# Prologue order, weight loads in pieces, one joint last projection and a mask moved between engines, in a recurrent-memory transformer kernel

## The chip, the core and the metric

The kernel runs on one core of a Trainium2 chip. A core has a matrix engine (TensorE, PE in the profile, whose weight loads are shown as PEld), VectorE (DVE), ScalarE (ACT), GpSimd (POOL) and SyncE (SP), which only issues transfers here. They run side by side and wait for each other by semaphores. The metric is the device time in microseconds (us) of one execution; smaller is better.

## The reference

The input x has 2048 tokens of width 448, in 64 segments of 32 tokens. Two layers of the same kind follow each other, each with a recurrent attention A and a gated feed-forward B:

```python
for s in range(n_seg):                               # A, 64 segments in order
    h = concat([mem, xs])                            # 8 memory rows + 32 tokens, L = 40
    q, k, v = h @ Wq, h @ Wk, h @ Wv                 # 16 heads of 256
    scores = q k^T * scale, masked (causal; the 8 memory keys are open to all)
    o = softmax(scores) v, then @ Wo                 # back to width 448
    mem = o[:8]; outs.append(o[8:])
# B: h = relu(x @ W_gate) * (x @ W_up); return h @ W_down     (448 -> 1792 -> 448)
x = x + A(layernorm(x)); x = x + B(layernorm(x))
x = x + A(layernorm(x)); x = x + B(layernorm(x))
```

The memory of a segment comes out of the one before, so the segments of a layer can't be done at once.

## The kernel before

**Prologue (lines 196 to 325).** For each pair of heads p (8 groups, `p4` of half `hf`) the products Wq Wk^T and Wv Wo are made once, as `A_sb` and `B_sb`. A block of 512 columns of Wq, Wk or Wv is loaded into one of six `nat` tiles by SP (`load_nat`), transposed on TensorE into `tpw` and copied to `qT`, `kT` or `vT` (`flips`, two halves for each). Copies out of PSUM are dealt out to VectorE and ScalarE by `share`. In the first loop over p each of the eight (kd, eo) positions has two `aps` products of 384 columns and two `mxw` products of 64, and the transposes for the next p (`todo`) are taken one by one after each kd, that is after positions 1, 3, 5 and 7 of 0 to 7. `first_rows` comes behind the third group. The second loop makes `B_sb` (`bps`). Behind it SP issues five loads of the feed-forward weights, `Wg_sb`, `Wu_sb` and `Wd_sb`.

**Steps (lines 505 to 661).** The layers are two chains of segments, the second `LAG` = 4 steps behind the first. `step(g)` handles segment g of chain 0 and segment g - 4 of chain 1, so steps 4 to 63 have both chains (full steps), 0 to 3 and 64 to 67 have one, and call 68 only projects. `xs` are the chains whose token output of the step before is projected in this step, `ms` those whose memory is needed next. A step projects its rows with `A_sb` (`prj`, evacuated to `TQ` and `TZ`), for the two halves of the heads, hf 0 and 1. The scores of the memory rows are `Sm`, those of the token rows `Sx`. The causal mask enters `Sx` as the first product of the accumulation:

```python
mm(Sp[:, :, :], ident[:], maskS[:], start=True, stop=False, skip_group_check=True)
```

`weights_of` makes the softmax on VectorE, with the exponential on ScalarE, out of `Sm` into `PM` and out of `Sx` into `PX`. `flipped` transposes those on TensorE (`pps`) and VectorE copies them to `PT`. `weigh_m` makes `ya` and `yb` from `PT` of the memory rows, `weigh_x` makes `y` from that of the token rows; both are evacuated to `Y`. `project_out` multiplies `Y` with `B_sb` into one PSUM tile `ox` of 80 columns, token rows of chain 0 in columns 0 to 31, memory in 32 to 47, token rows of chain 1 in 48 to 79, restricted to the columns `lo:hi` in use. It runs over t = 0 to 27 with four products each, and it is written in pieces between the other work:

```python
project_out(0, 0, 18)
probs_x(1, Sx1)
pm = flipped(PM[1], 1, "m1")
px0 = flipped(PX[0], 2, "x0")
project_out(0, 18, 21)
weigh_m(1, hk, pm)
```

Odd steps from 3 on also carry a feed-forward block (`Feed`: `residual`, `norm`, `xposed`, `gate_up` seven times, `down`, `norm2`, `feed_on`). Step 67 has chain 1 only and no `ms`: it projects the tokens of step 66, and call 68 those of step 67. `finish` copies the token columns of `ox` to `OT` and the memory back into `hT`. A last feed-forward block ends the kernel.

The order on TensorE is the order in which the program is written: `in_order` ties every matmul to the one before. The order on the other engines is made by the framework from the dependencies.

Of the kernel before, what the change touches and what calls it, by code (L numbers as in the profile page):

```python
# [23 lines left out]
FT = 14  # L24
# [8 lines left out]
HW = 4 * HI  # L33
W = 2 * L
XO = (0, 2 * L - SEG)
M0 = SEG
HX = (0, 64 + MEM)
HM = (SEG, 64)
# [15 lines left out]
def build_kernel(ctx, tc, A_x, A_mem0, A_Wq, A_Wk, A_Wv, A_Wo, B_W_gate, B_W_up, B_W_down, out,  # L54
# [141 lines left out]
    with tc.tile_pool(name="pre", bufs=6) as pre:  # L196
# [71 lines left out]
        for p in range(NP):  # L268
            hf, p4 = divmod(p, 4)
            qT, kT = ready  # L270
            ready, todo = queue(p + 1)
            mx_ps = psum.tile([P, 4, 128], F32, tag="ps", name="mxw")
            for kd in range(4):
                for eo in range(2):
                    aps = psum.tile([P, 3, 128], F32, tag="ps", name="aps")
                    for t in range(2):
                        e = 2 * eo + t
                        mm(aps[:, :, :], qT[:, e, kd * 128:(kd + 1) * 128],
                           kT[:, e, 0:384], start=(t == 0), stop=(t == 1))
                    for t in range(2):  # L280
                        e = 2 * eo + t
                        mm(mx_ps[:, kd, eo * 64:eo * 64 + 64], qT[:, e, kd * 128:(kd + 1) * 128],
                           kT[:, e, 384:448], start=(t == 0), stop=(t == 1))
                    t0 = eo * 4 + p4
                    if kd < 3:
                        share(A_sb[:, kd, hf, t0:t0 + 17:8, :], aps[:], 384, (1.28, 0.85))
                    elif upper(hf, eo):
                        share(A_sb[64:128, 3, hf, t0, :], aps[64:128, 0, :], 128, (1.28, 0.85))
                        share(A_sb[0:64, 3, hf, t0 + 8:t0 + 17:8, :], aps[0:64, 1:3, :], 256, (1.28, 0.85))
                    else:  # L290
                        share(A_sb[0:64, 3, hf, t0:t0 + 17:8, :], aps[0:64], 384, (1.28, 0.85))
                if todo:
                    todo.pop(0)()
            share(A_sb[:, 0:3, hf, 24 + p4, :], mx_ps[:, 0:3, :], 384, (1.28, 0.85))
            share(A_sb[0:64, 3, hf, 24 + p4, :], mx_ps[0:64, 3, :], 128, (1.28, 0.85))
            if p == 2:
                first_rows()
# [52 lines left out]
    Wg_sb = main.tile([P, 4, F], BF, name="Wg_sb")  # L350
    Wu_sb = main.tile([P, 4, F], BF, name="Wu_sb")
    Wd_sb = main.tile([P, FT, DM], BF, name="Wd_sb")
    for dst, src in ((Wg_sb, B_W_gate), (Wu_sb, B_W_up)):
        nc.gpsimd.memset(dst[64:128, 3, :], 0.0)
        nc.sync.dma_start(dst[:, 0:3, :], src[0:384].rearrange("(k p) n -> p k n", p=P))
        nc.sync.dma_start(dst[0:64, 3, :], src[384:448])
    nc.sync.dma_start(Wd_sb[:], B_W_down.rearrange("(f p) d -> p f d", p=P))

    class Feed:

# [115 lines left out]
    def queries(hf, g, kd):  # L476
        return TQ[hf][:, g, 2 * kd:2 * kd + 2, :] if kd < 3 else TZ[hf][:, g, :]

    def weights_of(Sp, n, dst, keep, tag):

        mx = main.tile([P, n], F32, tag=f"mx{tag}", name="mx")
        nc.vector.tensor_reduce(mx[:], Sp[:], axis=AX.X, op=ALU.max)
        se = main.tile([P, n, L], F32, tag=f"se{tag}", name="se")
        nc.vector.tensor_tensor(se[:], Sp[:], mx[:].unsqueeze(2).to_broadcast([P, n, L]), op=ALU.subtract)  # L484
        nc.scalar.activation(se[:], se[:], AF.Exp, scale=SCALE)  # L485
        ssum = main.tile([P, n], F32, tag=f"ssum{tag}", name="ssum")
        nc.vector.tensor_reduce(ssum[:], se[:], axis=AX.X, op=ALU.add)
        rs = main.tile([P, n], F32, tag=f"rs{tag}", name="rs")
        nc.vector.reciprocal(rs[:], ssum[:])
        if keep is not None:  # L490
            nc.vector.tensor_tensor(rs[:], rs[:], keep, op=ALU.mult)
        nc.vector.tensor_tensor(dst[:, :, 0:L], se[:], rs[:].unsqueeze(2).to_broadcast([P, n, L]), op=ALU.mult)
# [12 lines left out]
    def step(g, ff, pre):  # L505
# [4 lines left out]
        hb = hTb[gb % 2]  # L510
        cols = [(0, 32) if c == 0 else (48, 80) for c in xs] + [(32, 40) if c == 0 else (40, 48) for c in ms]
        lo, hi = min(a for a, _ in cols), max(b for _, b in cols)
        ox = psum.tile([P, 4, W], F32, tag="ox", bufs=1, name="ox")

        def hk_make():
            kps = psum.tile([P, 4, 128], BF, tag="ps", name="kps")
# [15 lines left out]

        def scores_x(hf):
            Sp = psum.tile([P, 4, L], F32, tag="ps", name="Sx")
            mm(Sp[:, :, :], ident[:], maskS[:], start=True, stop=False, skip_group_check=True)
            for half in range(2):
                for c in chains:
                    for kd in range(4):
                        mm(Sp[:, 2 * half + c, :], queries(hf, 3 * c + half, kd), moving(hb, j, kd, (c,)),
                           start=False, stop=(half == 1 and c == chains[-1] and kd == 3), skip_group_check=True)  # L540
            return Sp

        def probs_x(hf, Sp):
            weights_of(Sp, 4, PX[hf], None, f"x{hf}")

        def weigh_m(hf, hk, PT):
            if not ms:
# [11 lines left out]
        def weigh_x(hf, hk, PT, then=None):  # L559

            def keep(eng, c, t0, src):
                n = src.shape[-1] // SEG
                dst = YB[hf][:, t0:t0 + n, XO[c]:XO[c] + SEG]
                k = max(1, n // 8)
                evac(eng, dst.rearrange("p (k i) (e q) -> p k e i q", k=k, q=16),
                     src.rearrange("p (k e i q) -> p k e i q", k=k, e=2, q=16))

            y1 = {c: psum.tile([P, 512], F32, tag="ps", name=f"y1_{c}") for c in chains}
            for kd in range(2):
                for c in chains:  # L570
                    rows = slice(64 * c, 64 * c + L)
                    mm(y1[c][:, kd * 256:kd * 256 + 256], hk[rows, kd, :], PT[rows, 0:256], start=True, stop=True)
            for c in chains:
                keep(nc.scalar if c == 0 else nc.vector, c, 0, y1[c][:])
            y2 = {c: psum.tile([P, 384], F32, tag="ps", name=f"y2_{c}") for c in chains}
            for c in chains:
                rows = slice(64 * c, 64 * c + L)
                mm(y2[c][:, 0:256], hk[rows, 2, :], PT[rows, 0:256], start=True, stop=True)
            for eo in range(2):
                for c in chains:  # L580
                    rows = slice(64 * c, 64 * c + L)
                    mm(y2[c][:, 256:384], hk[rows, 3 + eo, :],
                       PT[rows, :].rearrange("p (e o w) -> p e o w", e=2, o=2)[:, :, eo, :],
                       start=(eo == 0), stop=(eo == 1))
            pre = then() if then is not None else {}
            for c in chains:
                keep(nc.scalar if c == 0 else nc.vector, c, 16, y2[c][:, 0:256])
                keep(nc.vector if c == 0 else nc.scalar, c, 24, y2[c][:, 256:384])
            return pre

        def project_out(hf, t0, t1):

            for t in range(t0, t1):
                for mc in range(4):
                    mm(ox[:, mc, lo:hi], B_sb[:, hf, t, mc * 128:(mc + 1) * 128],
                       YB[hf][:, t, lo:hi], start=(hf == 0 and t == 0 and mc == 0),
                       stop=(hf == 1 and t == NT - 1 and mc == 3), skip_group_check=True)

        def finish():
            if ms:  # L600
                src = ox[:, :, M0:M0 + 16].rearrange("p k (c m) -> p k c m", m=MEM)
                set_mem(g + 1, src[:, :, ms[0]:ms[-1] + 1, :], ms)
            o = (g - 1) % BLK * SEG
            for c in xs:
                o2 = o + (TB if c == 0 else 0)
                nc.scalar.copy(OT[:, :, o2:o2 + SEG], ox[:, :, XO[c]:XO[c] + SEG])
# [12 lines left out]
        project(0, chains, hb, j, (6, 0, 1), pre)  # L619
        if ff is not None:  # L620
            ff.residual()
        project(0, chains, hb, j, (2, 3, 4, 5))
        hk = hk_make()
        if ff is not None:
            ff.norm()
        project(1, chains, hb, j, (6, 0, 1))
        scores_m(0)
        project(1, chains, hb, j, (2, 3))
        if ff is not None:
            ff.xposed()  # L630
        project(1, chains, hb, j, (4, 5))
        pm = flipped(PM[0], 1, "m0")
        Sx0 = scores_x(0)
        weigh_m(0, hk, pm)
        scores_m(1)
        Sx1 = scores_x(1)
        probs_x(0, Sx0)
        feed(0, 1, 2)
        project_out(0, 0, 18)
        probs_x(1, Sx1)  # L640
        pm = flipped(PM[1], 1, "m1")
        px0 = flipped(PX[0], 2, "x0")
        project_out(0, 18, 21)
        weigh_m(1, hk, pm)
        feed(3, 4)
        project_out(0, 21, NT)
        feed(5, 6)
        weigh_x(0, hk, px0)
        if ff is not None:
            ff.down()  # L650
# [1 line left out]
        px1 = flipped(PX[1], 2, "x1")  # L652
        if ff is not None:
            ff.norm2()
        project_out(1, 16, 25)
        if ff is not None:
            ff.feed_on()
        project_out(1, 25, NT)
        finish()
        nxt = active(g + 1)  # L660
        return weigh_x(1, hk, px1, (lambda: project_early(nxt, hTb[(g + 1) // BLK % 2], (g + 1) % BLK)) if nxt else None)

# [75 lines left out]
```

## Time and profile before

| | |
|---|---|
| time, median of 3 runs | 1717.07 us (1716.97 to 1718.64) |
| profiled execution | 1716.17 us |
| span from its first to its last instruction | 1714.4 us |
| mean granted TensorE clock | 0.993 |
| matmuls | 41498 |
| DMA, mean | 33.17 MB, 19 GB/s |

The profile gives busy time of each engine, 40 slices of the span, the chain of work that ended last and groups of instructions. The trace can also be asked for stretches of time, for what each engine waited for, and for the instructions in order of time. "Waits for issue" are times in which an engine waited for nothing that the profile shows. A matmul's busy time holds its drain, which overlaps the next one, so its pace is read from the distance of two starts. The queues of the DMA part are q1 (hardware, issued by SP here), q0 (software, by POOL) and q8 and q14 (instructions).

### The profile page before, as it was taken

The numbers are of one execution on the slowest core, as the hardware profiler recorded it, in microseconds if no ns is written. First come the engines' busy times: TensorE is split into PE (matmuls) and PEld (weight loads), VectorE is DVE, ScalarE is ACT, GpSimd is POOL, SyncE is SP. The second block draws the span as 40 slices with busy tenths as digits, with TensorE's granted clock in tenths as the row PEclk, the third lists the DMA queues.
The fourth block names the chain that finished last, engine by engine and source line by source line (L and its number), as shares of the span: only waits on it lengthen the run. The fifth ranks groups of instructions, "written<-read, shape, count | busy, mean of one in ns | idle before, by whom it ended". The sixth has DMA issues, their size and how long they took to land.

```text
span 1714.4 us, 90663 instructions
## 1 busy us (share of the span) xinstructions
PE 1686.5 (98%) x41498; PEld 1589.5 (93%) x41498; DVE 1132.2 (66%) x3794; ACT 660.8 (39%) x1965; POOL 94.6 (6%) x202
## 2 busy tenths in 40 slices
PE   8989999999999999999999999999999999999998
PEld 6688999999999999999999999999999999999987
DVE  6656666676666666766666666766666667666664
ACT  5633333433333333343333334333333343433332
POOL 5300000000000000000000000000000000000000
PEclk9979999999999999999999999999999999999999
DMA  9520000000000000000000000000000000000000
GB/s 252 163 68 8 8 9 6 6 9 9 9 9 9 9 9 4 9 9 8 9 9 9 9 6 7 9 9 9 9 8 9 9 3 9 9 8 6 6 6 6
DMA packets 26623, 33.17 MB, mean 19 GB/s; under 512 B 3192, under 2 KB 24576, under 8 KB 26240
## 3 DMA queue, kind: packets, MB, share of 16 engines
q1 hardware_dynamic: 25152, 23.70, 5.0%
q8 instruction: 324, 5.31, 1.2%
q0 software_dynamic: 1088, 3.68, 0.7%
q14 instruction: 59, 0.48, 0.1%
HBM read 23.70 MB, written 1.84 MB: 15 GB/s over the span
## 4 chain that ended last, share of the span: by engine, by line
PE 96%; DVE 2%; issue 1%; ACT 1%; DMA 0%; POOL 0%; SPq 0%; POOLq 0%; DVEq 0%; ACTq 0%
PE ox L82 31%; PE prj L82 30%; PE ups L82 6%; PE gps L82 6%; PE dps L82 5%; PE y L82 4%; PE Sx L82 3%; PE pps L85 1%; PE bps L82 1%; PE tpw L85 1%; PE Sm L82 1%; PE aps L82 1%; PE ya L82 1%; PE tps L85 1%; PE yb L82 1%; PE kps L85 1%
## 5 line engine op out<-in xcount | busy, mean ns | idle before, releaser
L82 PE MATMUL ox<-Y,B_sb 128*128 128x80 bf16 (+4 forms) x15456 | 590.6, 199 | 1.5 <-issue 1.5
L82 PEld LDWEIGHTS <-B_sb 128*128 128x128 bf16 x15456 | 564.1, 99 | 10.2 <-issue 0.2
L82 PE MATMUL prj<-hT,A_sb 128*128 128x80 bf16 (+3 forms) x15232 | 569.5, 199 | 3.2 <-issue 3.2
L82 PEld LDWEIGHTS <-A_sb 128*128 128x128 bf16 (+1 forms) x15232 | 544.1, 99 | 7.8 <-issue 3.6
L89 ACT CAST TQ<-prj 128x320 bf16<-128x320 f32 (+1 forms) x456 | 169.9, 384 | 160.5 <-PE prj L82 128.5
L91 DVE CAST TQ<-prj 128x320 bf16<-128x320 f32 (+1 forms) x456 | 193.1, 431 | 44.9 <-PE prj L82 38.6
L91 DVE CAST Y<-y 128x128 bf16<-128x128 f32 (+2 forms) x384 | 162.2, 464 | 56.3 <-PE y L82 34.3
L89 ACT CAST Y<-y 128x512 bf16<-128x512 f32 (+2 forms) x384 | 144.2, 417 | 80.7 <-PE y L82 54.7
L396 DVE SCALAR_TENSOR_TENSOR hh<-gps,ut 128x256 bf16<-128x256 f32 (+1 forms) x238 | 95.6, 402 | 100.3 <-PE gps L82 93.6
L499 DVE COPY PT<-pps 128x128 bf16<-128x128 bf16 (+1 forms) x272 | 63.8, 255 | 120.2 <-PE pps L85 114.0
L82 PE MATMUL ups<-xT,Wu_sb 128*128 128x128 bf16 (+1 forms) x1904 | 140.0, 217 | 0.5 <-DVE xT L382 0.5
L82 PE MATMUL gps<-xT,Wg_sb 128*128 128x128 bf16 (+1 forms) x1904 | 140.0, 217 | 0.0
L395 ACT CAST ut<-ups 128x256 bf16<-128x256 f32 (+1 forms) x238 | 84.3, 355 | 105.5 <-PE ups L82 100.2
L557 ACT CAST Y<-yb 128x192 bf16<-128x192 f32 x134 | 42.6, 318 | 189.6 <-PE yb L82 189.0
L82 PEld LDWEIGHTS <-hk 40*128 40x128 bf16 (+1 forms) x1950 | 96.4, 95 | 16.9 <-issue 1.3
L82 PEld LDWEIGHTS <-Wg_sb 128*128 128x128 bf16 x1904 | 111.8, 98 | 0.0
L82 PEld LDWEIGHTS <-Wu_sb 128*128 128x128 bf16 x1904 | 109.5, 98 | 0.6 <-issue 0.6
L485 ACT ACTIVATE se<-se 128x80 f32<-128x80 f32 (+1 forms) x270 | 74.5, 299 | 90.0 <-DVE se L484 87.6
L160 POOL TENSOR_SCALAR rstd<-mv 128x1 f32<-128x1 f32 x67 | 14.8, 221 | 1554.1 <-DVE mv L158 1504.2
L82 PE MATMUL dps<-Wd_sb,hh 128*128 128x448 bf16 x476 | 95.9, 353 | 0.0
L82 PEld LDWEIGHTS <-TQ 128*128 128x128 bf16 x1938 | 86.8, 97 | 0.2 <-ACT TQ L89 0.2
L89 ACT CAST TZ<-prj 64x320 bf16<-64x320 f32 (+2 forms) x152 | 56.0, 378 | 74.2 <-DVE TZ L91 72.9
(112 smaller groups left out, 1801.1 us busy)
## 6 DMA issues: line engine op xcount, KB each, us to landing
wo<-in_A_Wo_dram POOLq DMA_DIRECT2D x8, 448.0 KB, 5.3
nat<-in_A_Wq_dram SPq DMA_DIRECT2D x8, 384.0 KB, 5.5
nat<-in_A_Wk_dram SPq DMA_DIRECT2D x8, 384.0 KB, 5.9
nat<-in_A_Wv_dram SPq DMA_DIRECT2D x8, 384.0 KB, 5.4
xa<-in_A_x_dram SPq DMA_DIRECT2D x32, 56.0 KB, 2.2
xa<-xp SPq DMA_DIRECT2D x32, 56.0 KB, 1.9
out_dram<-xa SPq DMA_DIRECT2D x32, 56.0 KB, 2.0
xp<-in_A_x_dram SPq DMA_DIRECT2D x30, 56.0 KB, 2.1
```

Source lines behind the costliest of these rows:

```text
L82: in_order(nc.tensor.matmul(*a, **k))
L85: in_order(nc.tensor.transpose(*a))
L89: nc.scalar.copy(dst, src)
L91: eng.tensor_copy(dst, src)
L160: nc.gpsimd.tensor_scalar(out=rstd[:], in0=mv[:, 1:2], scalar1=EPS, scalar2=None, op0=ALU.add)
L395: nc.scalar.copy(ut[:, :, n], ups[:, :, n])
L396: nc.vector.scalar_tensor_tensor(out=hh[:, 2 * u:2 * u + 2, n], in0=gps[:, :, n], scalar=0.0, in1=ut[:, :, n], op0=ALU.max, op1=ALU.mult)
L485: nc.scalar.activation(se[:], se[:], AF.Exp, scale=SCALE)
L499: nc.vector.tensor_copy(PT[:], pps[:].rearrange("p b q -> p (b q)"))
L557: nc.scalar.copy(YB[hf][:, 16:28, M0:M0 + 16], yb[:].rearrange("p (t q) -> p t q", q=16))
```

## The change

It has five parts.

- In the first prologue loop the transposes for the next group are taken after positions 0, 2, 4 and 5.
- The feed-forward weights are loaded in 15 pieces, `Wu_sb` first, each issued by `next_piece` from SP at five places of a step, behind the matmul that stands last in program order there; they are used up in steps 0, 1 and 2.
- Of `project_out(0, ...)`, 21 instead of 18 values of t stand ahead of the transposes of `PM[1]` and `PX[0]`, and 3 and 4 behind.
- In full steps the mask is no longer a product; VectorE adds `maskS` to `Sx` and writes the sum to `se`, out of which maximum and difference are then taken.
- Step 67 projects nothing; its token rows go into `Y` beside those of step 66 (columns 16 to 47), and call 68 projects both, 64 columns. The second copy to `OT` is made by VectorE. The unused transpose of `PM` in step 67 is left out.

```diff
+XL = 2 * L - 2 * SEG
...
-                if todo:
-                    todo.pop(0)()
+                    if todo and 2 * kd + eo in (0, 2, 4, 5):
+                        todo.pop(0)()
...
-    for dst, src in ((Wg_sb, B_W_gate), (Wu_sb, B_W_up)):
+    pieces = []
+    for dst, src in ((Wu_sb, B_W_up), (Wg_sb, B_W_gate)):
         nc.gpsimd.memset(dst[64:128, 3, :], 0.0)
-        nc.sync.dma_start(dst[:, 0:3, :], src[0:384].rearrange("(k p) n -> p k n", p=P))
-        nc.sync.dma_start(dst[0:64, 3, :], src[384:448])
-    nc.sync.dma_start(Wd_sb[:], B_W_down.rearrange("(f p) d -> p f d", p=P))
+        for k in range(3):
+            pieces.append((dst[:, k, :], src[128 * k:128 * k + 128]))
+        pieces.append((dst[0:64, 3, :], src[384:448]))
+    for f in range(0, FT, 2):
+        pieces.append((Wd_sb[:, f:f + 2, :], B_W_down[128 * f:128 * f + 256].rearrange("(f p) d -> p f d", p=P)))
+
+    def next_piece():
+        if pieces:
+            r = nc.sync.dma_start(*pieces.pop(0))
+            tc.add_manual_dep(r.ins, last_pe[0],
+                              mybir.DependencyInfo(mybir.DependencyClass.Sync,
+                                                   mybir.DependencyReason.DATA),
+                              reason="spread over the first steps")
...
-    def weights_of(Sp, n, dst, keep, tag):
+    def weights_of(Sp, n, dst, keep, tag, mask=None):
         mx = main.tile([P, n], F32, tag=f"mx{tag}", name="mx")
+        se = main.tile([P, n, L], F32, tag=f"se{tag}", name="se")
+        if mask is not None:
+            nc.vector.tensor_tensor(se[:], Sp[:], mask, op=ALU.add)
+            Sp = se
         nc.vector.tensor_reduce(mx[:], Sp[:], axis=AX.X, op=ALU.max)
-        se = main.tile([P, n, L], F32, tag=f"se{tag}", name="se")
...
+        end = g == nsteps - 1
+        if g == nsteps:
+            lo, hi = XL, XO[1] + SEG
...
-            mm(Sp[:, :, :], ident[:], maskS[:], start=True, stop=False, skip_group_check=True)
+            both = len(chains) == 2
+            if not both:
+                mm(Sp[:, :, :], ident[:], maskS[:], start=True, stop=False, skip_group_check=True)
...
-                           start=False, stop=(half == 1 and c == chains[-1] and kd == 3), skip_group_check=True)
+                           start=(both and kd == 0), stop=(kd == 3), skip_group_check=True)
...
-                dst = YB[hf][:, t0:t0 + n, XO[c]:XO[c] + SEG]
+                xo = XL if end else XO[c]
+                dst = YB[hf][:, t0:t0 + n, xo:xo + SEG]
...
         def project_out(hf, t0, t1):
+            if end:
+                return
...
+            if g == nsteps:
+                nc.scalar.copy(OT[:, :, 0:SEG], ox[:, :, XO[1]:XO[1] + SEG])
+                nc.vector.tensor_copy(OT[:, :, SEG:TB], ox[:, :, XL:XL + SEG])
+                return
...
         project(0, chains, hb, j, (6, 0, 1), pre)
+        next_piece()
         project(0, chains, hb, j, (2, 3, 4, 5))
...
         project(1, chains, hb, j, (6, 0, 1))
+        next_piece()
         scores_m(0)
...
-        pm = flipped(PM[0], 1, "m0")
+        pm = flipped(PM[0], 1, "m0") if ms else None
...
         feed(0, 1, 2)
-        project_out(0, 0, 18)
+        next_piece()
+        project_out(0, 0, 21)
         probs_x(1, Sx1)
-        pm = flipped(PM[1], 1, "m1")
+        pm = flipped(PM[1], 1, "m1") if ms else None
         px0 = flipped(PX[0], 2, "x0")
-        project_out(0, 18, 21)
+        project_out(0, 21, 24)
         weigh_m(1, hk, pm)
         feed(3, 4)
-        project_out(0, 21, NT)
+        project_out(0, 24, NT)
         feed(5, 6)
+        next_piece()
         weigh_x(0, hk, px0)
...
+        next_piece()
         project_out(1, 16, 25)
...
-        finish()
+        if not end:
+            finish()
```

More of the change, by code (lines that the diff above doesn't have):

```diff
@@ L512, in step @@
         lo, hi = min(a for a, _ in cols), max(b for _, b in cols)
-        ox = psum.tile([P, 4, W], F32, tag="ox", bufs=1, name="ox")
+        end = g == nsteps - 1
+        if g == nsteps:
+            lo, hi = XL, XO[1] + SEG
+        ox = psum.tile([P, 4, W], F32, tag="ox", bufs=1, name="ox") if not end else None
         def hk_make():
@@ L539, in scores_x @@
                         mm(Sp[:, 2 * half + c, :], queries(hf, 3 * c + half, kd), moving(hb, j, kd, (c,)),
-                           start=False, stop=(half == 1 and c == chains[-1] and kd == 3), skip_group_check=True)
+                           start=(both and kd == 0), stop=(kd == 3), skip_group_check=True)
             return Sp
         def probs_x(hf, Sp):
-            weights_of(Sp, 4, PX[hf], None, f"x{hf}")
+            weights_of(Sp, 4, PX[hf], None, f"x{hf}", maskS[:] if len(chains) == 2 else None)
         def weigh_m(hf, hk, PT):
```

## The prediction

> **What bounds the kernel now.** I read four views in this order: the page (which engine, where the slices are not full), the busy times of stretches, the waits of TensorE, and the timeline of one step. The page, on engines, slices and the chain:
>
> ```profile
> span 1714.4 us, 90663 instructions
> ...
> PE 1686.5 (98%) x41498; PEld 1589.5 (93%) x41498; DVE 1132.2 (66%) x3794; ACT 660.8 (39%) x1965; POOL 94.6 (6%) x202
> ...
> PEclk9979999999999999999999999999999999999999
> DMA  9520000000000000000000000000000000000000
> ...
> PE 96%; DVE 2%; issue 1%; ACT 1%; DMA 0%; POOL 0%; SPq 0%; POOLq 0%; DVEq 0%; ACTq 0%
> ```
>
> TensorE carries 96% of the chain, so time is won only by taking instructions off it or by ending its waits; slices 3 and 4 show a lowered clock and DMA load together. Stretches of steps 0, 1 and 2 (one chain each, nearly the same work) put a price on that:
>
> ```profile
> 81.46:102.97 21.51, 16.80 (x504) 16.01 (x504) 10.08 (x48) 6.24 (x27) 8.32 (x9) 0.66 0.63 191
> 102.97:120.72 17.75, 16.81 (x508) 16.04 (x507) 9.90 (x48) 6.45 (x27) 0.00 (x0) 0.83 0.02 4
> 120.72:136.64 15.92, 14.98 (x507) 14.28 (x504) 9.99 (x48) 6.63 (x28) 0.00 (x0) 1.00 0.02 5
> ```
>
> The columns are length, busy time of PE, PEld, DVE, ACT, POOL, granted clock, DMA share, GB/s. The same 504 to 508 matmuls take 21.51 us under 63% DMA load, then 17.75 at clock 0.83, then 15.92 undisturbed. The waits of TensorE over the whole span:
>
> ```profile
> PE pps L85 <- DVE PM L492: 4.5, 10, 0.8
> PE tps L85 <- DVE xn L170: 4.0, 3, 2.8
> PE prj L82 <- issue: 3.2, 1, 3.2
> PE aps L82 <- DVE kT L91: 2.0, 5, 0.4
> PE ox L82 <- issue: 1.5, 1, 1.5
> PE aps L82 <- ACT kT L89: 1.0, 2, 0.7
> ```
>
> Between 300 and 1600 us the same view is empty. It hides short waits, though: a matmul's busy time of about 0.2 us contains its drain, so I also took differences of starts from the records. The timeline of a step with both chains:
>
> ```profile
> 601.67 0.22 PE L85 MATMUL pps<-ident,PM 128*128 128x128 bf16 x1
> 601.73 0.23 PE L82 MATMUL Sx<-maskS,ident 128*128 128x160 bf16 x1
> ...
> 602.21 0.27 PE L82 MATMUL ya<-PT,hk 128*128 128x128 bf16 x2
> ```
>
> A mask product holds TensorE from its start to the next one's: 69 ns for hf 0, 72 ns for hf 1.
>
> **Part by part.** The sum goes against the profiled execution, 1716.17 us (span 1714.4); the median is 1717.07, 0.9 more, which I add at the end. About 0.2% (3.4 us) is what a measurement can tell from no change.
>
> *1. Transposes in the prologue.* At the start of each of eight groups p the second aps product waits for the last kT copy; starts show seven such waits, 0.48, five of 0.56 and 0.88, together 4.16 us. The new order ends the transposes after position 5 of 8, so the copy has two more products (2 x 0.383) and the next group's first transpose (0.447) before it is needed: 1.6 us, against 0.69 (VectorE) or 1.01 (ScalarE) for the copy. All seven waits should go. But groups become 4.85 instead of 5.41 us, and group 5 then begins at 34.4 and asks for its Wq block at 34.8, which before landed at 35.55 to 35.95, in a queue busy over 90% since the start. There TensorE waits about 1.0. I keep 0.4 for evacuations that now come closer together. Net -2.7; ends -4.2 (load earlier too) and -1.5.
>
> *2. Weights in 15 pieces.* In step 0 TensorE has two waits for issue, 3.35 and 1.66 us by starts. The instruction queue q8 moves 16 KB (256 instructions) each time; usually the next transfer starts with about 240 instructions in hand, but under the 4.7 MB of weights the one at 87.37 started only after TensorE had stopped at 86.93, and it resumed at 90.09. The clock then stood at 0.5 from 88.4 to 108.9. If all that went, steps 0 and 1 would become two of 15.92: 39.26 - 31.84 = -7.4. Two things come back. Step 0's 224 ox products have 8 columns, 3.3 ns of array work in 25 ns; with what lies between them that phase fills about 28% of the array's time over 7.9 us. The records show the clock dropped after a 3.4 us window filled to 35%, kept at 43%, and raised only by one near 100%. So I expect it to fall again and rise within step 1: projections at 35 instead of 25 ns for some 5 us (1.5) and 0.6 of transposes and y products: +2.1. And each 448 KB piece keeps the DMA busy for some 2 us (1344 KB took 6.7) of every 3, while 240 instructions at 25 ns a pair last 3.0 us and a fetch needs 2.2 to 2.7 from its start until TensorE goes on (1.0 to 1.1 of transfer, then 1.3 and 1.7 at the two stops); over 13 fetches I put +1.2, a guess inside its ends 0 and 5. SP's queue holds no load that anybody awaits behind the pieces: step 3's are next, and its first reader of these weights is gate_up there. Net -4.1; ends -7.4 and 0.
>
> The Trainium skill, "TensorE: Matmul & The Clock Gate", section on the HAM clock gate, says the clock falls after a whole idle window of some 3.4 us. The trace differs: it fell after a window with 1.5 us of idleness.
>
> *3. ox split 21/24 instead of 18/21.* In steps 0 to 3 and 66 the PM and PX transposes (or the ya behind them) wait for VectorE, 0.6 to 1.35 us. Twelve products of 25 ns move ahead of that wait: 5 x 0.3 = -1.5. In the 60 full steps nothing waits there: 0 by itself. Ends -1.8 and 0.
>
> *4. Mask on VectorE.* 60 steps with both chains lose two mask products: 60 x 69 ns and 60 x 72 ns, 8.4 us if both counted. The first does not. Behind it ya needs PT, VectorE's copy of the PM transpose: copy start 259 ns after that transpose, 225 long, ya 53 or 54 after its end, 537 in all, in every step; the last Sx before ya takes 31 instead of 25 ns, so ya already waits 6 ns. Taking 69 ns out ahead only lengthens that wait: 0. The second mask counts, behind Sx1 comes ox or gate_up: -4.3. VectorE gains two adds of 128x160 from PSUM per step; nearest row, se<-Sx,mx: 0.315 each, next start after 0.232. Walking the VectorE queue of a step without feed-forward (new order, old durations, 33 ns per semaphore), its last PX ends about 0.6 us later; behind it wait both PT copies and then ya of hf 1. That ya comes 0.36 us later (12 x 36 ns - 72) and had 60 ns to spare, so margin and delay nearly cancel: 20 ns left. In feed-forward steps six gate_up groups (2.7 us) cover it. I charge 30 steps x 27 ns = 0.8. Net -3.5; ends -4.3 and, with both adds as long as the 128x448 add of L374 (0.43 to the next start, +0.4 a step), +7.7.
>
> *5. The end.* Step 67 drops 224 ox products of 32 columns (1.82 + 0.30 + 0.71 + 1.62 + 1.30 = -5.74). They covered VectorE: PX was ready at 1681.99, gate_up ends at 1681.14, so px0 waits +0.9; px1's copy is bare, +0.55. The last 224 have 64 columns, 29 ns like ups of 64 instead of 25: +0.9. OT's second copy queues behind the first: +0.3. Net -3.1; ends -4 and -1, since the last clock window (low from 1702.9 to 1706.4) can fall worse.
>
> Sum: -2.7 - 4.1 - 1.5 - 3.5 - 3.1 = -14.9; 1716.2 - 14.9 + 0.9 = 1702.2, rounded to 1702.
>
> **Rivals.** (a) *Clock and fetch stay clean in the first steps.* Half-clock came only after a stop; steps 64 to 67 run at 43 to 75% without one. Term 2 is then -7.4: 1698.8. Against it: 8-column products fill far less. By the Trainium skill's rule above this is what happens. Chance 0.2. (b) *Pieces starve the fetch as the block did*, or the stops have another cause: term 2 is 0, 1706.2. For it: DMA is busy two thirds of these steps too. The Trainium skill, "Runtime: NRT & Kernel Launch", section Instruction fetch mechanics, holds fetches to be mostly hidden and TensorE's buffer to hold 2048 instructions; by it the load would not be the cause. The trace differs: TensorE stopped with the next 256 outstanding. Chance 0.16. (c) *Loads bind the whole prologue*, so earlier transposes only wait for Wq and Wk: term 1 is 0, 1704.8. Landings before were 1 to 4 us ahead, save in group 5. Chance 0.06. (d) *Slower: VectorE becomes the bound of the 30 full steps without feed-forward*, ya of hf 1 waiting for PT. It turns the whole into a loss once PT is (1717.1 - 1702.2)/30 = 0.5 us later still, beyond 0.2% at 0.61. Were an add as long as bn_stats (0.63 against 0.23), two would give 0.8 x 30 = +24: 1726. Softmax rows of that size are all 0.29 to 0.33, which speaks against it. Chance 0.05. (e) *Both masks count*, if PT comes early: 1698.0; the 53 ns in every step speak against it. Chance 0.05.
>
> **How the numbers follow.** The forecast itself has 0.48. Faster by over 0.2%: forecast, a, b, c, e and little of d, less what I overlooked: 0.91. Within 0.2%: 0.04, from the L374 end of term 4 (1702.2 + 11.2 = 1713.4). Slower: 0.05. The range 1696 to 1708.5 reaches past a, b, c and e and leaves out the upper end of term 4 and d.
>
> **What would show it.** Right: no mask products in full steps; ya of hf 0 still 53 ns behind PT, with a gap of some 75 ns after the last Sx; a pair of full steps 0.14 shorter than 48.58 us; groups of 4.85 us with one wait of about 1 us at the sixth; no issue wait over 1 us in step 0, a shorter half-clock stretch; last ox products at 29 ns. Wrong: PE waits on PT in the second half of steps without feed-forward, issue waits spread over steps 0 to 2, full steps 0.28 shorter a pair, or a prologue as long as before.

## The result and the profile after

The changed kernel took 1698.47 us (median of 4 runs, 1698.02 to 1699.25), the kernel before 1717.02 us beside it (1716.6 to 1718.64). The ratio is 0.9891, with a 95% interval of 0.9874 to 0.9908. The profiled execution took 1698.3 us. The page of the kernel after:

```profile
span 1696.5 us, 90084 instructions
...
PE 1675.2 (99%) x41152; PEld 1578.2 (93%) x41152; DVE 1165.0 (69%) x3919; ACT 669.1 (39%) x1958; POOL 94.6 (6%) x202
...
PEclk9989999999999999999999999999999999999999
DMA  9430000000000000000000000000000000000000
...
PE 96%; DVE 2%; ACT 1%; issue 0%; DMA 0%; POOL 0%; SPq 0%; POOLq 0%; DVEq 0%; ACTq 0%
```

TensorE still carries 96% of the chain, VectorE is busy 33 us longer, and "issue" has gone from 1% to 0%. The lowered clock is in slice 3 alone, at 8 tenths where it was at 7 (the page before has it in this slice alone too, and not in slice 4, as the prediction read it). Steps 0, 1 and 2 as stretches of the kernel after (length, busy time of PE, PEld, DVE, ACT, POOL, clock, DMA share, GB/s):

```profile
77.73:94.44 16.71, 16.15 (x509) 15.20 (x508) 10.30 (x49) 5.83 (x27) 8.31 (x9) 0.81 0.35 116
94.44:111.12 16.68, 16.05 (x509) 15.34 (x507) 9.90 (x48) 6.36 (x27) 0.00 (x0) 0.88 0.33 105
111.12:126.75 15.63, 14.99 (x509) 14.30 (x509) 9.99 (x48) 6.63 (x28) 0.00 (x0) 1.00 0.26 74
```

By these rows step 0 lost 4.8 us, step 1 1.1 and step 2 0.3. The border between steps 0 and 1 lies 0.3 us later here than in the rows before; with the same product as the border, the losses are 5.1 and 0.8. The DMA share, before 0.63 in step 0 alone, is now spread over three steps. The waits of TensorE after (engine and line, what it waited for, us in total, times, longest):

```profile
PE tpw L86 <- DMA nat<-in_A_Wq_dram: 5.7, 2, 5.5
...
PE pps L86 <- DVE PM L509: 3.5, 10, 0.8
PE y L83 <- DVE PT L516: 0.8, 1, 0.8
PE pps L86 <- DVE PX L509: 0.7, 1, 0.7
...
PE aps L83 <- ACT kT L90: 0.2, 1, 0.2
```

The waits for issue are gone and those of `aps` are down from 3.0 to 0.2 us. New are `pps` on `PX` and `y` on `PT`, in step 67, which the removed projection used to cover.

Stage lengths by differences of starts in the two traces, us, beside the terms of the prediction (number of the part, and its share):

| stage | before | after | change | term |
|---|---|---|---|---|
| start to the first aps | 9.27 | 9.70 | +0.43 | none |
| first prologue loop | 42.95 | 38.78 | -4.16 | 1: -2.7 |
| steps 0, 1 | 39.29 | 33.39 | -5.90 | 2: -4.1, with 0.6 of 3 |
| steps 2, 3, 66 | 55.80 | 54.67 | -1.13 | 3: -0.9 |
| steps 4 to 63 | 1452.68 | 1448.20 | -4.48 | 4: -3.5 |
| step 67 and the last ox | 26.42 | 23.73 | -2.70 | 5: -3.1 |

With +0.1 in the last feed-forward block these are the 17.9 us of the span; the prediction had 14.9.

### The profile page after: what moved, and what is told of

It is laid out like the page before. It is cut to its first block, busy times and chain, and to the rows that moved or that the text cites. A ratio compares the mean times of both kernels' runs of the same rounds, so it can differ in the third digit from the quotient of the medians.

```text
span 1696.5 us, 90084 instructions
## 1 busy us (share of the span) xinstructions
PE 1675.2 (99%) x41152; PEld 1578.2 (93%) x41152; DVE 1165.0 (69%) x3919; ACT 669.1 (39%) x1958; POOL 94.6 (6%) x202
## 4 chain that ended last, share of the span: by engine, by line
PE 96%; DVE 2%; ACT 1%; issue 0%; DMA 0%; POOL 0%; SPq 0%; POOLq 0%; DVEq 0%; ACTq 0%
PE ox L83 30%; PE prj L83 30%; PE ups L83 6%; PE gps L83 6%; PE dps L83 6%; PE y L83 4%; PE Sx L83 3%; PE pps L86 1%; PE bps L83 1%; PE tpw L86 1%; PE aps L83 1%; PE ya L83 1%; PE Sm L83 1%; PE tps L86 1%; PE yb L83 1%; PE kps L86 1%
## 5 line engine op out<-in xcount | busy, mean ns | idle before, releaser
L502 ACT ACTIVATE se<-se 128x80 f32<-128x80 f32 (+1 forms) x270 | 80.1, 303 | 104.4 <-DVE se L501 102.8
L83 PEld LDWEIGHTS <-hk 40*128 40x128 bf16 (+1 forms) x1950 | 100.2, 95 | 17.8 <-issue 1.7
L90 ACT COPY hT<-tps 128x256 bf16<-128x256 bf16 x32 | 11.9, 372 | 187.0 <-DVE hT L92 187.0
```

The lines of the kernel that those rows point to most:

```text
L83: in_order(nc.tensor.matmul(*a, **k))
L90: nc.scalar.copy(dst, src)
```

## The experiments

Each is the changed kernel with the edit shown. "No-feed steps" are the 30 full steps without feed-forward, "feed steps" the 30 with it; their mean lengths come from the records. The kernel before took 1716.0 to 1718.0 us beside these runs, so a change of the time by less than 2 us is read from the lengths of the steps, not from the time.

### Which mask product counted

```diff
-            both = len(chains) == 2
+            both = len(chains) == 2 and hf in (1,)      # e1: mask of hf 0 on TensorE again; e2: hf in (0,)
...
-            ... maskS[:] if len(chains) == 2 else None)
+            ... maskS[:] if len(chains) == 2 and hf in (1,) else None)
```

The first mask back on TensorE. 

> The changed kernel with the first mask (Sx of hf 0) in full steps back as a product on TensorE; the second stays an add on VectorE. Theory (ya of hf 0 is held by the PT copy, so the first mask product lay in a wait): full steps keep 19.384 us (even) and 28.890 us (odd), time 1698.5, within 0.7 of the changed kernel. Rival (every product taken off TensorE counts): 60 x 69 ns = +4.1, 1702.6.

The second mask back. 

> The changed kernel with the second mask (Sx of hf 1) back on TensorE; the first stays on VectorE. Theory (only the second product was on the path): 60 x 72 to 75 ns, +4.3 to +4.5, 1702.9, full steps back at 19.458 and 28.964 us. Rival (gain shared between the two masks, each worth half): +2.2, 1700.7. Rival (VectorE's lighter queue gives something back): under +4.

Measured: 1701.19 us (ratio to before 0.9904, 0.9889 to 0.9918) and 1701.79 (0.9908, 0.9893 to 0.9923). The first mask cost something after all. The mean steps say where:

| masks on TensorE | no-feed step | feed step |
|---|---|---|
| both (kernel before) | 19.458 | 28.964 |
| first only | 19.448 | 28.895 |
| second only | 19.401 | 28.965 |
| none (kernel after) | 19.384 | 28.890 |

In feed steps the first mask is free and the second costs 0.07 us, as predicted. In no-feed steps it is the other way about: the first costs 0.06, the second 0.01 to 0.02. The timeline of a no-feed step after (start, us, engine, line, operation, idle time before and its releaser) shows why:

```profile
831.96 0.22 PE L86 MATMUL pps<-ident,PM 128*128 128x128 bf16 x1
...
832.22 0.23 DVE L516 COPY PT<-pps 128x128 bf16<-128x128 bf16 x1
...
832.50 0.27 PE L83 MATMUL ya<-PT,hk 128*128 128x128 bf16 x2
...
832.61 0.32 DVE L498 TENSOR_TENSOR se<-Sx,maskS 128x160 f32<-128x160 f32 x1 [0.17 <-PE Sx L83]
...
832.85 0.41 DVE L574 CAST Y<-ya 128x256 bf16<-128x256 f32 x1
...
833.32 0.45 PE L83 MATMUL ox<-Y,B_sb 128*128 128x80 bf16 x8
```

`ya` starts 53 ns after the end of `PT`, as predicted. But behind it the first `ox` needs `Y`, VectorE's copy of `ya`, and that copy stands in VectorE's queue behind the add of the mask, which waits for the end of Sx0. `ox` starts 52 ns after the copy's end. With the first mask on TensorE, Sx0 ends one mask product later, and so does everything behind it:

```profile
833.68 0.22 PE L86 MATMUL pps<-ident,PM 128*128 128x128 bf16 x1
...
834.40 0.32 DVE L500 TENSOR_REDUCE mx<-Sx 128x4 f32<-128x160 f32 x1 [0.24 <-PE Sx L83]
...
834.65 0.41 DVE L574 CAST Y<-ya 128x256 bf16<-128x256 f32 x1
...
835.11 0.48 PE L83 MATMUL ox<-Y,B_sb 128*128 128x80 bf16 x9
```

From `pps` to `ox` it is 1.43 us here against 1.36. The second mask product costs so little here since it lies in the wait that `ox` has anyway: the first `ox` starts 79 ns after the last product of Sx1 without it, and 25 ns after it in the run of the second mask. In feed steps gate_up comes in between, and no `ox` waits.

### Ending the wait of ya

```diff
                 for kd in range(3 if u in pre else 4):
+                    if mid is not None and u == us[-1] and p4 == 3 and kd == 1:
+                        mid()                  # PM of hf 0 transposed three products earlier
```

> The changed kernel with the transpose of PM (hf 0) three products (107 ns) earlier, inside the last projection unit, so that PT is ready 107 ns earlier against Sx. Theory (the PT copy holds ya): ya of hf 0 no longer waits after the last Sx, 60 x 69 to 75 ns = -4.1 to -4.5 in full steps, and 7 single-chain steps gain some 0.07 each: 1693.7. Rival (PM is not ready so early, or the PT copy stands behind a TQ cast on VectorE): between 0 and -2, with the wait moved to the transpose or the copy.

Measured: 1698.14 us (0.9885, 0.9869 to 0.9902), against 1698.47 nothing that can be told apart. No-feed steps took 19.384 as before, feed steps 28.869. `ya` did come 75 ns earlier, but in no-feed steps the copy of `ya` started no earlier (9.251 us into the step in both), since the add ahead of it still waited for Sx0. In feed steps the first memory score of hf 1 to Sx1 took 0.05 longer; the ScalarE copy of the last `TQ` came 55 ns later and ended 0.135 us ahead of the first of these products instead of 0.216. I take it for the cause, but it was not tried alone. So the wait is one of several that lie close behind each other. The next experiment takes two at once, in no-feed steps only:

```diff
+        early = len(chains) == 2 and ff is None     # the earlier transpose in these steps alone
...
-            nc.vector.tensor_copy(YB[hf][:, 0:16, M0:M0 + 16], ...)
+            evac(nc.scalar if hf == 0 and len(chains) == 2 and ff is None else nc.vector, YB[hf][:, 0:16, M0:M0 + 16],
+                 ...)
```

> In full steps without feed-forward the transpose of PM for hf 0 is taken three products earlier and ya of hf 0 is copied by ScalarE instead of VectorE. Theory (what the first ox product of such a step waits for is VectorE's copy of ya, queued behind the add of the mask, which itself waits for the end of Sx0; the earlier transpose alone gave 0 there because of that queue): the first ox follows Sx1 within 0.06 us, these 30 steps go from 19.384 to 19.30 us, time 1696.0. Rival (ScalarE's copy is as late as VectorE's, or ox waits for something else): these steps stay at 19.384 within 0.02, time 1698.5. Steps with feed-forward 28.890 by both.

Measured: 1698.06 us (0.9893, 0.9878 to 0.9908), no-feed steps 19.370. The first `ox` followed Sx1 at once and stood 0.13 us earlier in the step, so the theory of VectorE's queue holds. Yet 0.12 of it came back in hf 1 of the same step:

```profile
835.79 0.18 DVE L508 RECIPROCAL rs<-ssum 128x4 f32<-128x4 f32 x1
835.80 0.22 PE L86 MATMUL pps<-ident,PM 128*128 128x128 bf16 x1
...
836.00 0.32 DVE L511 TENSOR_TENSOR PX<-se,rs 128x160 bf16<-128x160 f32 x1
836.24 0.41 DVE L518 COPY PT<-pps 128x128 bf16<-128x128 bf16 x2
...
836.51 0.27 PE L83 MATMUL ya<-PT,hk 128*128 128x128 bf16 x2
```

TensorE reaches the transpose of `PM` 0.13 earlier, but VectorE is still on the softmax of hf 1: `PX` stands ahead of `PT`, which starts 0.44 us after the transpose instead of 0.26 to 0.29. VectorE sets the pace here, rival (d) in a mild form.

The next two runs carry the edit above and more: step 0 with wide columns (below), `ff.xposed()` between the transpose of `PM` and Sx0 in feed steps, and in step 67 the `PX` transposes moved; the second of them also this:

```diff
-        pm = flipped(PM[1], 1, "m1") if ms else None
+        pm = flipped(PM[1], 1, "m1", nc.scalar if early else None) if ms else None   # PT copied by ScalarE
```

> The changed kernel with four edits: step 0 projects into columns 0 to 39, full steps without feed-forward as in the run with the copy on ScalarE, full steps with feed-forward take the transposes of xn (tps) between the transpose of PM and Sx0, and step 67 takes the transposes of PX two gate_ups later (hf 0) and before the down products (hf 1). Theory: clock kept in steps 0 and 1 (-1.2), 30 x -0.085, 30 x -0.07 since four transposes now cover the wait of ya for PT, and two waits of 0.9 and 1.0 us in step 67 gone: 1698.4 - 1.2 - 2.5 - 2.1 - 1.9 = 1690.7. Rival (each wait is handed on to VectorE's queue, as with the earlier transpose alone): only the clock and step 67 count, 1695.3.

> The combined run with one edit more: in full steps without feed-forward the copy of PT of the memory rows of hf 1 is made by ScalarE. Theory (VectorE runs its softmax chain without a gap from the end of Sx0 to the last PX of such a step, so when TensorE was freed of the waits for ya and ox of hf 0, 0.13 us ahead of pps, that time was given back as a wait of ya of hf 1 for a PT copied behind PX; 0.115 us a step): these 30 steps go from 19.369 to 19.255 us, time 1690.0. Rival (ScalarE's copy comes as late, or y waits for VectorE's next copy instead): 19.369 within 0.02, time 1693.5.

Measured: 1693.47 us (0.9866, 0.9849 to 0.9882) and 1690.44 (0.9849, 0.9834 to 0.9863). Feed steps went to 28.82, no-feed steps from 19.369 to 19.251 with the last edit:

```profile
832.21 0.22 PE L86 MATMUL pps<-ident,PM 128*128 128x128 bf16 x1
...
832.41 0.33 DVE L511 TENSOR_TENSOR PX<-se,rs 128x160 bf16<-128x160 f32 x1
832.47 0.27 ACT L90 COPY PT<-pps 128x128 bf16<-128x128 bf16 x1 [0.65 <-PE pps L86]
...
832.81 0.28 PE L83 MATMUL ya<-PT,hk 128*128 128x128 bf16 x2
```

`PT` no longer stands behind `PX`, and `ya` comes 0.60 us after the transpose, with the twelve `ox` products between them at their full pace. Step 67 gained 1.27 us and not 1.9: 0.34 came back as a wait of gate_up for `ut`, and 0.16 was lost ahead of Sx.

### The first steps: clock and loads

```diff
+        if g == 0:
+            lo = 0                              # ox of step 0 over 40 columns instead of 8
```

> The changed kernel with the ox products of step 0 made 40 columns wide (columns 0 to 39, of which 0 to 31 multiply zeros and are not read) instead of 8; the issue pace stays 25 ns. Theory (the clock falls because narrow products fill too little of the array): no half clock in steps 0 and 1, step 0 and 1 at 15.6 each instead of 16.71 and 16.68, -2.1, time 1696.4. Rival (the clock falls on waits for PM and PT in the step, or on the step's low count of products): half clock for some 10 us as before, 0.

Measured: 1697.25 us (0.988, 0.9866 to 0.9895). Steps 0 and 1, columns as above:

```profile
78.36:93.87 15.51, 14.97 (x509) 14.34 (x508) 10.30 (x49) 5.73 (x26) 8.31 (x9) 1.00 0.40 115
93.87:109.98 16.11, 15.15 (x509) 14.37 (x509) 10.04 (x48) 6.45 (x27) 0.00 (x0) 1.00 0.38 116
```

As many products, the same order, only wider moving operands, and the clock stays at 1.00. So it was the little-filled array that took it away, 1.8 us in these two steps. It stays in all five profiles of runs with 40 columns in step 0, and falls in all seven with 8 columns and the loads in pieces. The time fell by 1.2 only; the first prologue loop took 0.57 us longer in this profile. Step 1 is 0.4 longer than step 2: it has a wait for issue of 0.6 us, and step 2 one of 0.4.

The five big loads again, before step 0:

```diff
-            pieces.append(...)                  # 15 pieces
+        nc.sync.dma_start(dst[:, 0:3, :], ...)  # Wg, Wu and Wd at once, as before the change
```

> The changed kernel with the feed-forward weights again in five loads before step 0, gate first. Theory (the loads starve TensorE's instruction fetch, and the two stops and the half clock behind them are the cost): waits for issue of some 3.4 and 1.7 us come back in step 0, the clock is at one half for about 20 us, steps 0 and 1 become 38.7 us together instead of 33.4, time 1703.8. Rival (the stops had another cause, and the gain came from the new order in these steps): steps 0 and 1 stay at 33.4 within 0.5, time 1698.5.

Measured: 1704.22 us (0.9925, 0.991 to 0.994), steps 0 and 1 21.82 and 16.47. Its waits of TensorE between 75 and 120 us:

```profile
PE prj L83 <- issue: 2.6, 1, 2.6
PE ox L83 <- issue: 2.1, 1, 2.1
PE pps L86 <- DVE PM L507: 0.6, 2, 0.3
```

The two stops are back, and so is the half clock, though for 13.7 us, most of them in step 0, where the kernel before had 20 over two steps. The transfers of the instruction queue q8 end at 85.12 and 92.01 us, and TensorE starts again 1.4 us behind each, at 86.56 and 93.40; so it was instructions that it waited for. Whether the smaller waits for issue also come from loads was tried last, by leaving step 1 without any (five pieces in steps 0 and 2, three in step 3, with `Wd_sb` in five pieces instead of seven, on top of the next section's kernel):

```diff
-        next_piece()
+        if g != 1:
+            next_piece()
```

> The run with the kept clock at the end, and no weight piece issued in step 1: five pieces in step 0, five in step 2, three in step 3, Wd in five pieces of three blocks (the last of two) instead of seven of two. Theory (the issue waits of 1.0 to 1.3 us seen in step 1 of the runs at full clock are instruction fetches that share the DMA engines with the pieces): no issue wait in step 1, which takes 15.65 us instead of 16.41, and at most 0.3 us of them in steps 2 and 3; time 1687.4. Rival (they come from the way the steps' instructions are consumed, whatever else the DMA does): step 1 stays at 16.2 to 16.7, time 1688.1. If the waits come under the pieces of step 2 instead, the pieces are the cause and the time stays.

Measured: 1687.06 us (0.9828, 0.9811 to 0.9844), 1.1 below the run that it is built on. Step 1 took 15.64 us instead of 16.39, but step 2 16.14 instead of 15.68. The waits for issue, which the run that it is built on had in steps 1 and 2 (0.9 and 0.4 us, and not in step 1 alone, as the expectation has it), were in steps 2 and 3 (0.8 and 0.2), at 114.7 and 131.2 us. The first ended 1.3 us behind a transfer of q8 (114.38 us). Waits of TensorE from 75 to 155 us:

```profile
PE pps L86 <- DVE PM L512: 1.6, 5, 0.4
PE prj L83 <- issue: 1.1, 2, 0.8
...
```

This is the outcome named last in the expectation, and it speaks for the pieces as the cause: step 3 has such a wait in no other profile, and the two profiles without pieces in steps 1 and 2 (the kernel before and the run with five loads) have none there. It is one profile, though. Of the eleven with pieces in step 1, eight have waits for issue, 0.8 to 1.3 us in all, mostly in steps 1 and 2; three have none, the changed kernel's above among them. The 1.1 us are no gain of these waits: the spans of the two profiles are 1685.6 and 1685.1 us, and the four runs of the one that it is built on lie between 1686.9 and 1688.9. Their cause stays open.

### The prologue

```diff
-                    if todo and 2 * kd + eo in (0, 2, 4, 5):
-                        todo.pop(0)()
+                if todo:
+                    todo.pop(0)()
```

> The changed kernel with the transposes of the first prologue loop taken after positions 1, 3, 5 and 7 again. Theory (each of seven groups waits 0.48 to 0.88 us for the last kT copy, and the shorter groups never waited for a Wq load because that load's issue is tied to the transposes and moved with them): the loop goes from 38.78 to 42.95 us, the Wq block of group 6 is issued 2 us later, time 1702.6. Rival (part of the gain was the load's timing by chance): 41.4 us, time 1701.1.

Measured: 1704.23 us (0.9929, 0.9915 to 0.9944); the waits are those of before again:

```profile
...
PE aps L83 <- DVE kT L92: 2.0, 5, 0.4
PE aps L83 <- ACT kT L90: 1.0, 2, 0.7
...
```

The loop took 44.58 us, 1.6 more than before the change; that part lies in its first group (7.27 us against 5.64), where the clock rose at 13.9 us instead of 9.9. The other groups are as before, 5.41 where the new order gives 4.85.

### The end

```diff
-        end = g == nsteps - 1
+        end = False                             # two last projections, 32 columns each
```

> The changed kernel with the joint last projection undone: step 67 projects the tokens of step 66 (32 columns), call 68 those of step 67 (32 columns), both copies to OT by ScalarE. Theory (stage lengths of the two profiles: step 67 3.9 us longer, the ox products of call 68 1.2 shorter, nothing else): time 1701.2. Rival (the joint projection also moved the clock windows at the end and gained or lost there): 1700 or 1703.

Measured: 1702.06 us (0.9917, 0.99 to 0.9934). Step 67 is 3.86 us longer, the last ox 1.22 shorter: 2.64. The rest of the 4.1 us between the spans of the two profiles is not shown to be the projection's: 0.65 lies in the last gate_ups, with the clock at half for 6.8 us there instead of 3.4 (as also in the profiles of the second mask and of the prologue, which have the joint projection), and 0.63 in a wait for the Wq load of the sixth prologue group.

```diff
+    warm(3)                                     # products of 512 columns that nobody reads
     ff.residual()
+    warm(10)
     ff.norm()
     ff.xposed()
+    warm(2)
```

> The run with PT on ScalarE and 15 extra products of 128x128 by 128x512 whose results nobody reads, 3 behind the last ox, 10 behind the last otp and 2 behind the last tps, each within a time in which TensorE waits. Theory (the clock falls there since a window of 3.4 us is filled to 0.06 to 0.18, and the next one runs the gate_up products at half pace): clock 1.0 up to the down products, the last gate_ups 1.4 us shorter, time 1688.6. Rival (the extra products hold up the transposes behind them, or the clock falls all the same): 1690 to 1690.8.

Measured: 1688.12 us (0.9835, 0.982 to 0.985), 2.3 below the run that it is built on. The end of its timeline:

```profile
1671.43 2.32 PE L83 MATMUL dm<-B_sb,ident 128*128 128x512 bf16 x10
1674.35 0.44 PE L86 MATMUL tps<-ident,xn 128*128 128x128 bf16 x4 [0.60 <-DVE xn L171]
1674.62 0.60 PE L83 MATMUL dm<-B_sb,ident 128*128 128x512 bf16 x2
1675.30 0.39 PE L83 MATMUL ups<-xT,Wu_sb 128*128 128x64 bf16 x8
1675.53 0.40 PE L83 MATMUL gps<-xT,Wg_sb 128*128 128x64 bf16 x8
```

`tps` still waits for `xn`, so the extra products hold nobody up, and eight products of 64 columns take 0.23 us each time. First `ups` to first `dps` is 3.26 us instead of 4.81. Another 0.5 is in step 67, where neither the wait of gate_up for `ut` nor the loss ahead of Sx occurred; why is open.

## Why the prediction was right, point by point

The forecast, 1702 us, was 3.5 too slow; the sign of every term held, and 1698.5 is inside the range. The time alone can't tell the forecast from rivals (a), 1698.8, and (e), 1698.0. Against (a), the clock did fall; against (e), a pair of full steps became 0.148 us shorter, where 0.14 was forecast and 0.28 would have been both masks. Part of the 3.5 is luck of this execution: a wait for the Wq load and waits for issue, priced at 1.0 and 1.2 us, did not come here, but came in 5 of 12 (0.1 to 1.0 us) and 8 of 11 profiles (0.8 to 1.3) with the same code in these places.

**Term 1, -2.7, measured -4.16.** The cause was right: seven waits gone, groups of 4.85 us. Mis-sized was the new wait at the sixth group. I took the landing times of before as given, 35.55 to 35.95, but the load's issue moves with the transposes that free its tile: at 22.21 instead of 24.23 us, landed 34.17 to 34.95. With the same prologue code that wait was 0.98 us in one later profile (landed at 36.19 us), 0.63 in another and 0 in seven of twelve: it comes and goes with the landing. The 0.4 for evacuations did not show.

**Term 2, -4.1, measured about -5** (5.9 less the 0.6 that term 3 forecast for these steps; the run with five loads, which takes this part back alone, lost 4.9 in them). The clock's part held: 2.1 predicted, and steps 0 and 1 take 33.39 where twice step 2 is 31.26. It fell at 88.1 us after a window of 3.4 us filled to 0.29 (columns moved at 0.42 ns each, the pace of the 512-column products above, whose starts are 0.216 us apart) and rose at 98.4. The 1.2 for fetches under the pieces did not come in this profile; the runs since have 0.8 to 1.3 us of them in most profiles, so the guess was of the right kind.

The rule of the Trainium skill ("TensorE: Matmul & The Clock Gate", the HAM clock gate), that the clock falls after an idle window, does not account for the run of 40 columns: neither run had an idle window there (the longest pause between two starts in the window of the fall was under 0.45 us), and only one lost the clock. The Trainium skill, "Runtime: NRT & Kernel Launch", Instruction fetch mechanics, has fetches mostly hidden; the run with big loads does not agree, at 4.7 us of stops.

**Term 3, -1.5, measured -1.1 for the 0.9 forecast in steps 2, 3 and 66.** Steps 2 and 66 lost 0.30 and 0.31, step 3 0.52. Its 0.6 in steps 0 and 1 could not be told from term 2, and no run took this part back alone.

**Term 4, -3.5, measured -4.48.** Right for feed steps (0.072 predicted, 0.074 measured). In no-feed steps the step that failed is "the first mask counts nothing". I followed Sx0 to `ya` and stopped there; `ox` behind it waited on VectorE's queue, and through it on the end of Sx0. The 27 ns charged for VectorE's delay were not paid: `PT` of hf 1 started 26 ns late, with `ya` 92 to 96 ns behind it where 53 is the least. The real 74 ns of a no-feed step is about 60 of the first mask and 10 to 17 of the second. That both kinds of step lost 74 ns, by different masks, is chance. Rival (e), both masks in full, is out; rival (d) holds as a limit that lies just behind, and (b) and (c) fell by the runs of the loads and of the prologue.

**Term 5, -3.1, measured -2.70.** `pps` on `PX` 0.94, as said; `y` on `PT` 1.01 instead of 0.55, since VectorE's add of the down products stood ahead of the copy:

```profile
1672.08 0.28 PE L86 MATMUL pps<-ident,PX 128*128 128x128 bf16 x2
...
1672.28 0.61 DVE L425 TENSOR_TENSOR xa<-dps,xa 64x448 bf16<-64x448 f32 x1 [1.95 <-PE dps L83]
...
1672.82 0.27 DVE L516 COPY PT<-pps 128x256 bf16<-128x256 bf16 x1
...
1673.14 0.60 PE L83 MATMUL y<-PT,hk 40*128 40x256 bf16 x5 [0.79 <-DVE PT L516]
```

## What to carry to other kernels

Follow a removed instruction through every queue that its end releases, not only to the next wait on its own engine: TensorE's first `ox` waited for a copy that stood behind an add that waited for the product. Where two engines run close to each other, one wait removed gives the next one; three edits together (an earlier transpose, two copies on ScalarE) gave 0.13 us a step, the first alone nothing and the first two 0.01. And take an operation's load or fetch wait from several executions, since such waits came and went here by 1 us with the same code around them.

## What the hardware showed that was not expected

- The clock went by how full the array was, as the prediction had it, and not by idle windows. With 8-column products it fell after a window filled to 0.29; with 40 columns, of which 32 are never read (0.53 and more), it stayed. Fifteen products of 512 columns in waits at the end kept it in a place where windows had held 0.06 to 0.18.
- Loads in flight can stop TensorE for instructions: 4.7 us under five big loads; under pieces 0.8 to 1.3 us in nine of twelve profiles and nothing in three. In the one profile with no pieces in step 1 the wait in it was gone, and one in step 3 came up.
- The best version run, 1687.06 us, is 29.4 us below the kernel before beside it (1716.5), and 11.4 below the changed kernel. Of these 11.4, 6.1 come out of the full steps, though the page of the changed kernel calls TensorE 99% busy.
